# Four query buffers in place of two in a two-branch attention kernel, with a re-dealt instruction plan

## The chip, the cores and the metric

The kernel runs on one core of a Trainium2 chip. The metric is the device time of one execution in microseconds (us). The kernel before took 821.07 us, the median of 7 runs (819.73 to 822.99).

## What is computed

The input x is 2048 tokens by 512 features, bf16. Two attention branches of 32 heads of 16 features each read it; a gate mixes their outputs.

```python
g = sigmoid((x * gate_w).sum(-1))
# A: softmax attention
q, k, v = split(x @ A_wqkv)                       # 32 heads x 16
o = softmax(q k^T * 16**-0.5) v
a = o @ A_wo
# B: linear attention with the softmax feature map phi(u) = [softmax(u w_phi), softmax(-u w_phi)]
q, k, v = split(x @ B_wqkv)
kv, z = phi(k)^T v, sum(phi(k))
b = ((phi(q) kv) / (phi(q) z + 1e-6)) @ B_wo
out = g * a + (1 - g) * b
```

Branch A is nearly all of the work: 32 heads x 2048 x 2048 exponentials.

## The kernel before

**Rounds.** Branch A's work is cut into 32 rounds, numbered n: four chunks of 512 queries by eight groups of four heads. A round has 16 key tiles of 128 keys, and for each key tile four scores (one per head), each a 128 x 512 tile: 64 score tiles in a round.

**Two paths for a score tile.** Of the 16 key tiles of a round, DVE_COUNT[n] (1 to 4) go to VectorE and GpSimd, the others to ScalarE.

- ScalarE's path: two score matmuls (L934, a pair) write two of the four banks of `ps_ring`; one exponential over both (L952) writes two of the NSLOT = 22 slots of the ring ET; four matmuls with the value tile (L991, called PV below) add into `ps_ot`. The score pair k waits for exponential k-2, whose banks it takes. An exponential waits until the PV matmuls that read its slots have run, NSLOT tiles back.
- VectorE's path (`dve_pack`): score matmuls (L1041) into banks of `ps_mp`; VectorE converts them into EW (L1046); the fraction is converted into Ef (L1075, on POOL or VectorE as the plan decides), the exponent into ED (L1079, POOL); VectorE computes a polynomial (L1084, L1086, L1088); a DMA from POOL's queue adds Ef into ED (L1091); four PV matmuls (L1102) read ED.

At the end of a round VectorE transposes `ps_ot` (L1131), divides (L1133, L1134) and, after each second round, transposes into onT_A (L1142).

**Query buffers.** The scores need the queries of a round as four zero-padded planes, one per head, with 16 live rows each. Two rounds share one projection (L775), copied into one of two staging buffers qst (L792); `place_qT` then issues four DMA copies on SP's queue (L810), which put each head's 16 rows into the buffer of that round. There are two such buffers, `qT[:, n % 2]`, cleared once by VectorE at the start (L729). The copies for round n wait for the last score pair of round n-2 (`qk_last`) and for the last VectorE-path score of round n-2 (`qk_dve`), both of which read the same buffer. For the first two rounds VectorE makes the planes itself (L796).

**Branch B and the projections** fill the gaps: features are computed by a projection, two exponentials on ScalarE (phi, L1250), a DMA transpose on SP's queue (phiT, L1285), sums, a reciprocal and products on VectorE. `phi` has six buffers. Outputs of the first three query chunks are projected (L1345), scaled on VectorE into one of three `outt` buffers (L1366) and stored (L1353).

**The order of the work** comes from a planner in the kernel (`Sched`), which runs when the program is built. Each operation has an engine, an assumed duration, a priority and a due time; a greedy loop deals them to the five engines and so fixes each engine's instruction list and every semaphore wait. The tables at the top of the file (LEAD, AFF, PAIR, JOINT, OFF, PRI, SHY, FILL, SLIP, POLY, SHAPE, mostly one value per round) shift priorities, release times and choices in it. Where PE would idle by over 0.26 us in the plan, and fewer than QUOTA = 4700 columns were streamed in the last TICK = 3.413 us of it, the planner puts in spare matmuls (L1010) that multiply a zero tile, so that PE stays busy:

```python
while (self.open and now - t[e] > self.SPARE and
       sum(n for x, n in self.recent if x > now - self.TICK) < self.QUOTA):
    z = self.spare(cfg)
```

Of the kernel before, what the change touches and what calls it, by code (L numbers as in the profile page):

```python
# [11 lines left out]
P = 128  # L12
D = 512
H = 32
DH = 16
S = 2048
NT = S // P
QCH = 512
# [10 lines left out]
NSLOT = 22  # L29

PASSES = 1
LEAD = [30.0, 5.0, 15.587634343078882, 19.4910031759405, 21.09664890476773, 40.82165272376692, 4.700229106743385, 13.0]
PACE = [1.0771457571608845, 0.4579007635970128]
BOUNDS = [3.0710501327799653, 8.000889564597248, 8.026121532808418, 18.02257936663145, 29.86797202712817]
# [4 lines left out]
AFF = [4.39977984498405, 3.9999969024869326, 0.0709056182711651, 2.610626798369437, 0.0, 3.8238247132441265, 0.2373548188763579, 1.6727442850838754, 0.0, 0.6573637706948927, 0.11081142926777193, 1.5407840050620647, 0.0, 3.3884248072966137, 0.44709012098761747, 1.0475205744010385, 0.6221806062526727, 0.0, 0.9703265408840219, 3.181313389852499, 2.9697049628010324, 0.0, 0.4901783546835013, 0.0, 0.0, 2.786126368892715, 1.0743845299433354, 0.7132921107694127, 3.722000841705053, 4.3096284141584125, 0.22230757516151967, 2.6591770654809825, 0.0]  # L39
PAIR = [1, 0, 0, 0, 0, 1, 0, 0, 0, 0, 1, 1, 0, 1, 1, 1, 1, 1, 0, 1, 1, 1, 0, 0, 0, 1, 0, 0, 1, 0, 1, 0, 0]  # L40
JOINT = [0, 0, 1, 0, 0, 0, 0, 1, 1, 1, 0, 0, 0, 0, 0, 0, 1, 1, 1, 1, 1, 1, 1, 1, 0, 0, 0, 0, 1, 1, 1, 1, 0]
SWD = [0.65, 662500, 1.85]
CLEAR = [3.0, 1.2, 0.97, 4.85, 3.2623642462425315, 5.2, 2.6, 0.05]
OFF = [0.0, 0.7641466610336427, 0.5172481291637241, 5.004931148448025, 1.7040388526462977, -7.164186188736442, 0.7559066313969969, 1.9941725662135408, -6.707776703782448, 4.972788778180723, 5.007934767851205, -6.13598057955875, 3.881877451844217, -2.647081027044541, -5.72687170676355, -0.22403507521855937, -4.84468290973168, 4.404669149906992, 7.812513114609348, 3.1840076962397728, -6.5688103099769055, 0.35249872570063623, 3.345678581583612, -4.520043988488846, -1.9086060678527623, 10.430360554436882, 3.604407185155254, -16.81889329298839, 4.746243695454299, -2.846662271061698, 5.685383556076899, 5.689588100027095, 0.0]
PRI = [-2.5977761809841518, 7.675212586195942, 3.895376356683779, 19.79515516194705, -7.3276780691927526, 14.469014115627996, 8.592499852018925, 14.099502747418079, 12.338502872342715, 1.7122892583984095, -8.935875976393678, 0.5395473944292624, 14.23703340786056, 3.2346729790774353, 0.3457488045955195, 0.08236959814205402, -17.48520710204307, -7.161052481135956, -16.754409768115014, -4.23626845606058, 7.608907873204804, -3.2170380366050266, 8.401619955625353, -20.005512559792166, 1.3250396846988832, 4.674069890641421, -7.994912686036253, -4.543452568119845, 2.6005386807691826, -5.230522475232639, -10.205604389261005, 0.3055335737033076, 0.0]
SHY = [0.9001243968886534, 1.8374205889246058, 0.0, 2.3537546061047485, 0.18257087375037662, 1.4295929945532806, 0.0, 0.5036278855954646, 0.6445455027631356, 0.2763577403328745, 1.1375351044326518, 2.139068753246887, 0.8637774561861942, 0.0, 1.3587360146178078, 1.1498488277746914, 4.411308196696776, 1.5770165321690843, 0.0, 1.9277987030895938, 0.9106226852257446, 1.1437315353611544, 0.5739539000045727, 0.1122566866758205, 2.0455679537055595, 0.8660155278776578, 0.6489629968075317, 3.2915775917012993, 0.0, 0.0, 0.1739731045745717, 1.0328008471107046, 0.5]
FILL = [0.008114156552610996, 0.8711172814468358, 0.1337127379043423, 0.6175020065897155, 0.7705201692590595, 0.3506528409175884, 0.2044338913945295, 0.5026251860805567, 0.5, 0.21748892677719284, 0.48467810123534716, 0.3196791772769674, 0.2851905504944167, 0.01919447461597057, 0.15335430645841516, 0.32782401328955907, 0.2084505307424424, -0.011934960453968912, 0.520663695866737, 0.5981936577952663, 0.11372240291845498, 0.6724825225634218, 1.0685006718840102, 0.5449804341491988, -0.3447736801528881, 0.360791111116348, 0.09588691498317847, 0.029755556837955832, 0.29038499291635267, 0.6891067868200518, 0.5206497795807705, 0.1370411081981146, 0.5]
SLIP = [0.020288650601543372, 0.020525550031210083, 0.06075207595460803, 0.0, 0.0, 0.0, 0.13508451326551305, 0.0, 0.024065167618767248, 0.0, 0.015945258750116847, 0.0, 0.002841362237768881, 0.05233800887856601, 0.0, 0.0, 0.0554960908741312, 0.014128492530835347, 0.06406254955060428, 0.01059294453046039, 0.06237810720540699, 0.14637347669762, 0.0, 0.03425975512431642, 0.07117502284429342, 0.0852953029317602, 0.0, 0.016465068465927216, 0.0, 0.11752530161540813, 0.10555114660507484, 0.0, 0.0]
POLY = [2.5698857428809108, 0.8749370011032089, -0.8991089305608342, -3.284378557461031, -2.104961201961929, 2.1622309334875944, -1.9547520224875896, 1.9344506377095603, 0.8679101929667505, 6.980907311200291, 0.597989766211239, 11.29232777066949, 4.7841112088256725, 3.454905016185241, -9.642279457647597, -1.4127995308506685, -1.3053317023544437, -1.7341301539172118, 7.659960632132543, 5.984807460007567, 4.8208000760169565, 0.5343684926269039, 5.3604542710823715, -0.36855426206960495, 0.9175715562645521, 1.9673598560009513, -4.573797529614719, 1.399931277308983, -4.6711373321518534, -0.22371921092667524, 3.420996744961034, 5.649687125694619, 2.3718927004339707]
SHAPE = [0, 1, 2, 0, 3, 2, 1, 0, 0, 4, 0, 0, 3, 0, 0, 3, 0, 0, 1, 1, 0, 0, 1, 1, 3, 0, 1, 2, 0, 0, 1, 4, 1]  # L50
# [11 lines left out]
DVE_COUNT = (1, 3, 4, 3, 3, 3, 2, 2, 1, 3, 3, 4, 2, 4, 3, 3, 3, 3, 4, 3, 4, 3, 2, 4, 3, 3, 3, 3, 3, 3, 3, 4)  # L62
# [61 lines left out]
class Sched:  # L124
# [330 lines left out]
    TICK, QUOTA = 3.413, 4700  # L455
# [56 lines left out]
class _Kernel:  # L512
# [43 lines left out]
    def memory(self):  # L556
# [20 lines left out]
        bf, f32 = dt.bfloat16, dt.float32  # L577
# [22 lines left out]
        at("qT", [P, 2, 4, QCH], bf)  # L600
# [17 lines left out]
        at("outt", [P, 3, D], bf)  # L618
        at("phi", [P, 6, H, 2, DH], bf)
# [9 lines left out]
    def pools(self):  # L629
        self.mp = BufPool(NMP)  # L630
        self.mp.scarce = True
        self.qst_p = BufPool(2)
        self.onTA_p = BufPool(9)
        self.onTB_p = BufPool(9)
        self.EW_p = BufPool(2)
        self.ED_p = BufPool(3)
        self.Ef_p = BufPool(3)
        self.outt_p = BufPool(3)
        self.phi_p = BufPool(6)
        self.VB_p = BufPool(6)  # L640
        self.phiT_p = BufPool(2)
        self.fs_p = BufPool(2)
        self.ob_p = BufPool(2)
# [10 lines left out]
    def bank(self, readers=1):  # L654
        return Buf(self.mp, readers)
# [63 lines left out]
    def consts(self):  # L719
        s = self.s  # L720
# [9 lines left out]
                     for n in range(2)]  # L730
# [8 lines left out]
        for k in range(WARM + 5):  # L739
# [5 lines left out]
            if 0 <= t < 4:  # L745
# [6 lines left out]
                if t % 2:  # L752
# [4 lines left out]
                    else:  # L757
# [7 lines left out]
                             order=[self.o_iden])  # L765
# [38 lines left out]
    def place_qT(self, n):  # L804
        par = n % 2
        st, o_ev = self.st_q[n // 2]

        def put(i):
            r0 = 32 * i + 16 * par
            return lambda e: e.dma_start(self.qT[r0:r0 + 16, par, i, :], self.qst[r0:r0 + 16, st.idx, :])  # L810
        self.o_qT[n] = [self.s.op(
            "sp", 2.45, [put(i) for i in range(4)],
            [o_ev, self.qk_last.get(n - 2), self.qk_dve.get(n - 2), self.o_qz[par]], self.tn(n) - LEAD[4], dma=65536,
            frees=[st])]
        self.o_qT[n][0].lat = 2.3
        self.o_qT[n][0].kind = "qT"
# [63 lines left out]
    def main_chain(self):  # L880
# [28 lines left out]
        for k, (ua, ub) in enumerate(groups):  # L909
# [20 lines left out]
            def qk(x, half):  # L930
                n, kt, i = units[x]
                g = SEQ[n][1]
                r = slice(64 * (i // 2), 64 * (i // 2) + 64) if half else slice(0, P)
                return lambda e: e.matmul(  # L934
                    self.ps_ring[:, x % RING, :], self.kT[r, g // 2, kt * P:(kt + 1) * P],
                    self.qT[r, n % 2, i, :], start=True, stop=True, tile_position=(r.start, 0))
# [82 lines left out]
    def dve_pack(self, n, kt, first_pv):  # L1019
# [19 lines left out]
        def score(i, bank, half):  # L1039
            r = slice(64 * (i // 2), 64 * (i // 2) + 64) if half else slice(0, P)  # L1040
            return lambda e: e.matmul(  # L1041
                bank(), self.kT[r, cp, kt * P:(kt + 1) * P], self.qT[r, n % 2, i, :], start=True, stop=True,
                tile_position=(r.start, 0))
# [392 lines left out]
```

## Time and profile before

The profile is of one execution, whose own time was 823.03 us and whose span (first to last instruction of the core) is 821.2 us.

| what | before |
|---|---|
| median of 7 runs | 821.07 us (819.73 to 822.99) |
| profiled execution, its span | 823.03 us, 821.2 us |
| busy PE / VectorE (DVE) / ScalarE (ACT) / GpSimd (POOL) | 748.8 / 758.5 / 802.4 / 394.9 us |
| exponentials ET (L952), phi (L1250) | 834, 64 |
| spare matmuls (L1010) | 383 |
| start of the first and last ET | 8.8, 812.8 us |

A row of a group reads: line, engine, operation, output<-input by name, partitions x elements and type, count, then busy time in us and the mean ns of one, then the idle time of the engine just before these instructions and what ended it. A row of the timeline has the start and the length of a merged piece in us, and in brackets the idle time ahead of it with its releaser. A row of the chain of waits has start, length and what it was. PE's matmuls overlap, so their durations add to more than the time they hold the engine. DVE is VectorE, ACT ScalarE, POOL GpSimd, SP the queue engine; "SPq" is SP issuing a DMA.

### The profile page before, as it was taken

The page shows a single profiled execution, that of the slowest core. Times are in us where ns is not written, and L with a number is a line of the kernel's source. Part 1 is how long each engine was busy: PE and PEld are TensorE (multiplying, and loading weights), DVE is VectorE, ACT ScalarE, POOL GpSimd, SP SyncE. Part 2 cuts the span into 40 slices and gives each one's busy share as a digit, 9 for nine tenths or more (in the row PEclk, how much of TensorE's full clock was granted, in tenths as well). Part 3 has the DMA queues.
Part 4 walks back from the last instruction along what each step waited for, and adds up shares of the span by engine and source line. Part 5 has one row for each costly group of instructions (what it writes and reads, how often), then busy time and mean ns, then how long its engine had stood idle before and what let it go on. Part 6 is the DMA issues. An engine that isn't in the chain of part 4 may idle for free.

```text
span 821.2 us, 14918 instructions
## 1 busy us (share of the span) xinstructions
PE 748.8 (91%) x5944; PEld 225.4 (27%) x5944; DVE 758.5 (92%) x1124; ACT 802.4 (98%) x906; POOL 394.9 (48%) x435
## 2 busy tenths in 40 slices
PE   8999999999999889898999998888888988888997
PEld 3333232333333223222222222222222222222222
DVE  7999999998699999999999999999799999898893
ACT  6999999999999999999999999999899999999997
POOL 3436434632124546556555455544455555564450
PEclk9999999999999999999999999999799999999999
DMA  5454434353326436246534534445356445444433
GB/s 124 115 103 105 88 74 87 73 111 76 69 54 145 95 78 112 59 100 124 103 81 100 115 82 87 94 93 117 72 104 119 81 88 91 84 77 81 81 71 84
DMA packets 96598, 75.84 MB, mean 92 GB/s; under 512 B 76817, under 2 KB 84369, under 8 KB 96529
## 3 DMA queue, kind: packets, MB, share of 16 engines
q0 software_dynamic: 13680, 49.81, 30.8%
q1 hardware_dynamic: 81360, 24.42, 14.5%
q8 instruction: 47, 0.77, 0.4%
q10 hardware_dynamic: 1488, 0.66, 0.3%
q14 instruction: 23, 0.18, 0.1%
HBM read 3.69 MB, written 2.10 MB: 7 GB/s over the span
## 4 chain that ended last, share of the span: by engine, by line
ACT 81%; DVE 7%; PE 6%; DMA 3%; POOL 1%; issue 1%; SPq 0%; POOLq 0%
ACT ET L952 77%; ACT phi L1250 3%; DVE EW L1046 2%; DMA ED<-Ef 2%; PE ps_ring L934 2%; DMA qT<-qst 1%; PE ps_ot L991 1%; DVE Ef L1088 1%; DVE Em L1084 1%; PE ps_mp L1041 1%; DVE Em L1086 1%; DVE Wp L1182 1%; PE ps_mp L1345 1%; PE ps_mp L775 1%; PE ps_ot L1102 0%
## 5 line engine op out<-in xcount | busy, mean ns | idle before, releaser
L952 ACT ACTIVATE ET<-ps_ring 128x1024 bf16<-128x1024 f32 x834 | 776.4, 1214 | 6.9 <-PE ps_ring L934 4.7
L934 PE MATMUL ps_ring<-qT,kT 64*128 64x512 bf16 x1668 | 328.8, 388 | 55.2 <-ACT ET L952 44.6
L1079 POOL TENSOR_SCALAR ED<-EW 128x512 int16<-128x512 int16 (+2 forms) x240 | 221.6, 951 | 197.3 <-DVE Em L1084 49.9
L1046 DVE TENSOR_SCALAR EW<-ps_mp 128x512 int32<-128x512 f32 (+1 forms) x288 | 237.7, 852 | 24.8 <-PE ps_mp L1041 19.3
L934 PEld LDWEIGHTS ps_ring<-qT,kT 64*128 64x128 bf16 x1668 | 80.5, 93 | 327.6 <-ACT ET L952 311.4
L1091 POOL DMA_DIRECT2D ED<-Ef x95 | 87.5, 924 | 123.3 <-DVE Ef L1088 67.6
L991 PE MATMUL ps_ot<-ET,Vaug 128*17 128x512 bf16 x1668 | 146.7, 385 | 0.0
L1075 POOL TENSOR_SCALAR Ef<-EW 128x1024 f16<-128x1024 uint16 (+1 forms) x93 | 88.4, 951 | 89.9 <-DVE EW L1046 28.2
L1088 DVE TENSOR_TENSOR Ef<-Ef,Em 128x2048 int16<-128x2048 f16 x95 | 120.7, 1271 | 0.6
L1084 DVE TENSOR_TENSOR Em<-Ef 128x2048 f16<-128x2048 f16 x95 | 120.5, 1269 | 0.5
L1041 PE MATMUL ps_mp<-qT,kT 64*128 64x512 bf16 (+1 forms) x380 | 102.3, 385 | 7.9 <-DMA qT<-qst 2.6
L1010 PE MATMUL ps_ot<-zero,iden 64*128 64x512 bf16 (+1 forms) x383 | 88.9, 379 | 0.0
L1075 DVE TENSOR_SCALAR Ef<-EW 128x1024 f16<-128x1024 uint16 (+1 forms) x131 | 79.3, 617 | 0.1
L1086 DVE TENSOR_SCALAR Em<-Em 128x2048 f16<-128x2048 f16 x95 | 68.7, 723 | 0.3
L991 PEld LDWEIGHTS ps_ot<-ET,Vaug 128*17 128x17 bf16 x1668 | 32.0, 87 | 74.3 <-issue 68.1
L775 PE MATMUL ps_mp<-Wp,xT 128*128 128x512 bf16 x128 | 41.6, 385 | 0.0
L1250 ACT ACTIVATE phi<-ps_mp 128x512 bf16<-128x512 f32 x64 | 40.0, 778 | 1.3 <-PE ps_mp L775 1.3
L1102 PE MATMUL ps_ot<-ED,Vaug 128*17 128x512 bf16 x380 | 37.5, 385 | 2.1 <-DMA ED<-Ef 1.9
L775 PE MATMUL ps_mp<-xT,WA 128*128 128x512 bf16 (+1 forms) x128 | 38.5, 378 | 0.6 <-ACT phi L1250 0.3
L1041 PEld LDWEIGHTS ps_mp<-qT,kT 64*128 64x128 bf16 (+1 forms) x380 | 27.1, 94 | 40.8 <-DVE EW L1046 18.7
L1010 PEld LDWEIGHTS ps_ot<-zero,iden 64*128 64x128 bf16 (+1 forms) x383 | 25.9, 94 | 11.3 <-issue 0.3
L1131 DVE STREAM_TRANSPOSE T<-ps_ot 128x512 f32<-128x512 f32 x31 | 21.9, 708 | 2.6 <-PE ps_ot L991 2.5
(93 smaller groups left out, 410.9 us busy)
## 6 DMA issues: line engine op xcount, KB each, us to landing
ED<-Ef POOLq DMA_DIRECT2D x95, 512.0 KB, 4.5
qT<-qst SPq DMA_DIRECT2D x120, 16.0 KB, 1.9
out_dram<-outt SPq DMA_DIRECT2D x12, 128.0 KB, 2.0
WA<-in_A_wqkv_dram SPq DMA_DIRECT2D x3, 384.0 KB, 4.5
phiT<-phi SPq DMA_TRANSPOSE x48, 3.1
WBV<-in_B_wqkv_dram SPq DMA_DIRECT2D x1, 512.0 KB, 4.6
Wp<-in_A_wo_dram SPq DMA_DIRECT2D x1, 512.0 KB, 4.1
WBV<-in_B_wo_dram SPq DMA_DIRECT2D x1, 512.0 KB, 4.9
```

Source lines behind the costliest of these rows:

```text
L775: m = s.op("pe", self.c_mm(n), lambda e, c=c: e.matmul(self.bk(b)[:, 0:n], lhs(c), rhs(c), start=(c == 0), stop=(c == 3)), deps if c == 0 ...
L934: return lambda e: e.matmul(self.ps_ring[:, x % RING, :], self.kT[r, g // 2, kt * P:(kt + 1) * P], self.qT[r, n % 2, i, :], start=True, st ...
L952: self.o_exp.append(s.op("act", w * 0.434 + 0.039, lambda e, b0=b0, s0=s0, w=w: e.activation(self.ET[:, s0:s0 + w, :], self.ps_ring[:, b0: ...
L991: return lambda e: e.matmul(self.ps_ot[32 * i:32 * i + VSL, :], self.Vaug[:, kt, h, :], self.ET[:, (4 * p + k) % NSLOT, :], start=(kt == 0 ...
L1010: return lambda e: e.matmul(self.ps_ot[c:c + nc, :], self.iden[r:r + nr, 0:nc], self.zero[r:r + nr, :], start=False, stop=False, tile_posi ...
L1041: return lambda e: e.matmul(bank(), self.kT[r, cp, kt * P:(kt + 1) * P], self.qT[r, n % 2, i, :], start=True, stop=True, tile_position=(r. ...
L1046: return s.op("dve", dur, lambda e: e.tensor_scalar(self.EW[:, ew.idx, x * QCH:(x + w) * QCH].rearrange("p (b q) -> p b q", b=w) if w > 1 else
L1075: fs = [s.op("pool", U * 8.26e-4 + 0.28, lambda e, c=c: e.tensor_scalar(self.Ef[:, ef.idx, U * c:U * c + U], half(0, dt.uint16, c, U), flo ...
L1079: hs = [s.op("pool", W * 8.26e-4 + 0.165, lambda e, c=c: e.tensor_scalar(self.ED[:, ed.idx, W * c:W * c + W].bitcast(dt.int16), half(1, dt ...
L1084: u = s.op("dve", 1.13, lambda e: e.tensor_tensor(self.Em[:], Ef(), Ef(), ALU.mult), fs + [self.ed_prev], pr, port=True)
L1088: g_ = s.op("dve", 1.13, lambda e: e.tensor_tensor(Ef().bitcast(dt.int16), Ef(), self.Em[:], ALU.mult), [q], pr, port=True)
L1091: v = s.op("pool", SWD[0], lambda e: e.dma_start(out().bitcast(dt.int16), Ef().bitcast(dt.int16), accum_op=ALU.add), [g_] + hs, pr, frees= ...
```

## The change

There are four query buffers in place of two: round n uses `qT[:, n % 4]`, and its copies wait for rounds n-4. The two new buffers are cleared by POOL at the start. To make room, ET has 20 slots in place of 22, `phi` five buffers in place of six, `outt` two in place of three. QUOTA goes from 4700 to 4100. DVE_COUNT moves one key tile from round 3 and one from round 11 to rounds 6 and 30 (95 in all in both). The plan tables get new values in some entries: AFF 9, PAIR 5, JOINT 10, OFF 8, PRI 10, SHY 7, FILL 14, SLIP 12, POLY 9, SHAPE 12 of 33 each, LEAD and BOUNDS one each. The planner's code is the same, so the order of the instructions on every engine is dealt anew. Lines after the clearing of the buffers stand two lower in the changed file (L952 is L954 there).

```diff
-NSLOT = 22
+NSLOT = 20
...
-DVE_COUNT = (1, 3, 4, 3, 3, 3, 2, 2, 1, 3, 3, 4, 2, 4, 3, 3, 3, 3, 4, 3, 4, 3, 2, 4, 3, 3, 3, 3, 3, 3, 3, 4)
+DVE_COUNT = (1, 3, 4, 2, 3, 3, 3, 2, 1, 3, 3, 3, 2, 4, 3, 3, 3, 3, 4, 3, 4, 3, 2, 4, 3, 3, 3, 3, 3, 3, 4, 4)
...
-    TICK, QUOTA = 3.413, 4700
+    TICK, QUOTA = 3.413, 4100
...
-        at("qT", [P, 2, 4, QCH], bf)
+        at("qT", [P, 4, 4, QCH], bf)
...
-        at("outt", [P, 3, D], bf)
-        at("phi", [P, 6, H, 2, DH], bf)
+        at("outt", [P, 2, D], bf)
+        at("phi", [P, 5, H, 2, DH], bf)
...
-        self.outt_p = BufPool(3)
-        self.phi_p = BufPool(6)
+        self.outt_p = BufPool(2)
+        self.phi_p = BufPool(5)
...
         self.o_qz = [s.op("dve", 0.9, lambda e, n=n: e.memset(self.qT[:, n], 0.0), prio=-200 + 101 * n)
-                     for n in range(2)]
+                     for n in range(2)] + [
+            s.op("pool", 2.6, lambda e, n=n: e.memset(self.qT[:, n], 0.0), prio=-97 + n, order=[self.o_iden])
+            for n in (2, 3)]
...
-            return lambda e: e.dma_start(self.qT[r0:r0 + 16, par, i, :], self.qst[r0:r0 + 16, st.idx, :])
+            return lambda e: e.dma_start(self.qT[r0:r0 + 16, n % 4, i, :], self.qst[r0:r0 + 16, st.idx, :])
         self.o_qT[n] = [self.s.op(
             "sp", 2.45, [put(i) for i in range(4)],
-            [o_ev, self.qk_last.get(n - 2), self.qk_dve.get(n - 2), self.o_qz[par]], self.tn(n) - LEAD[4], dma=65536,
+            [o_ev, self.qk_last.get(n - 4), self.qk_dve.get(n - 4), self.o_qz[n % 4]], self.tn(n) - LEAD[4], dma=65536,
             frees=[st])]
```

In the score matmuls (L934, L1041) `self.qT[r, n % 2, i, :]` becomes `self.qT[r, n % 4, i, :]`.

## The prediction

> **What bounds the kernel.** I read the page's busy table first, then the groups, then ScalarE's row of the timeline for its pauses, then the chain of waits through the longest pause, then the table by stretches for the TensorE clock there.
>
> ```profile
> span 821.2 us, 14918 instructions
> ...
> PE 748.8 (91%) x5944; PEld 225.4 (27%) x5944; DVE 758.5 (92%) x1124; ACT 802.4 (98%) x906; POOL 394.9 (48%) x435
> ...
> L952 ACT ACTIVATE ET<-ps_ring 128x1024 bf16<-128x1024 f32 x834 | 776.4, 1214 | 6.9 <-PE ps_ring L934 4.7
> ...
> L1010 PE MATMUL ps_ot<-zero,iden 64*128 64x512 bf16 (+1 forms) x383 | 88.9, 379 | 0.0
> ```
>
> ScalarE is busy 98% of the span with 834 exponentials (ET) and 64 feature exponentials (phi), so only what makes ScalarE pause can be won. The busy share hides some of it: an ET lasts 1214 ns but the next begins sooner. From the trace's start times, the median step from ET to ET is 0.904 us and a phi's 0.478. So 833 x 0.904 + 64 x 0.478 + 0.13 for the two gate exponentials = 783.7 us; from the first ET (8.78) to the last (812.80) are 804.0. ScalarE loses **20.3 us** inside its own stream; 8.8 lie ahead and 8.4 behind. The excess of each step over 0.904 tells where: 4.7 us at 574.6 to 585.7; 0.8 at 626.7; 3.7 in the early part (1.8 at 143.1, 0.7 at 101.3, 0.4 at 159.5, 0.9 in three between 65 and 71); 0.9 at 463; 0.7 at 710; the rest in some hundreds of small ones, of which the largest (0.1 to 0.3 each) stand where one round of queries follows the other.
>
> The longest, first as ScalarE's pauses, then as the chain of waits:
>
> ```profile
> 577.74 1.94 ACT L952 ACTIVATE ET<-ps_ring 128x1024 bf16<-128x1024 f32 x2 [1.88 <-PE ps_mp L1041]
> 580.09 1.02 ACT L952 ACTIVATE ET<-ps_ring 128x1024 bf16<-128x1024 f32 x1 [0.42 <-PE ps_ring L934]
> 581.60 1.02 ACT L952 ACTIVATE ET<-ps_ring 128x1024 bf16<-128x1024 f32 x1 [0.48 <-PE ps_ring L934]
> 582.88 1.02 ACT L952 ACTIVATE ET<-ps_ring 128x1024 bf16<-128x1024 f32 x1 [0.25 <-PE ps_ring L934]
> 584.38 1.02 ACT L952 ACTIVATE ET<-ps_ring 128x1024 bf16<-128x1024 f32 x1 [0.48 <-PE ps_ring L934]
> ```
>
> ```profile
> 569.54 0.34 PE ps_ring L934 x2
> 569.88 0.10 SPq L810
> ...
> 572.50 4.12 DMA qT<-qst
> 576.62 0.05 issue
> 576.66 0.61 PE ps_mp L1041
> ```
>
> A score pair of two rounds earlier ends at 569.88; only then may SP's queue issue the four copies into that round's query buffer; the last lands at 576.62, and PE, idle until then, begins the next round's scores. The 626.7 loss is the same wait (PE idle 0.80 us, released by qT<-qst). Why the ETs stay late until 585.7 is in the table by stretches (columns: PE, weight loads, DVE, ACT and POOL busy, granted clock, DMA share, GB/s):
>
> ```profile
> 572.38:575.80 3.42, 2.32 (x12) 0.50 (x9) 3.42 (x7) 3.42 (x4) 0.52 (x1) 1.00 0.78 155
> 575.80:579.22 3.42, 2.56 (x15) 0.55 (x15) 1.53 (x3) 1.54 (x3) 1.48 (x3) 0.50 0.25 49
> 579.22:582.63 3.41, 3.41 (x17) 0.76 (x13) 2.94 (x6) 2.51 (x3) 1.81 (x3) 0.50 0.59 115
> 582.63:586.05 3.42, 3.42 (x20) 0.89 (x20) 1.56 (x4) 2.44 (x3) 2.36 (x4) 0.50 0.58 115
> 586.05:589.50 3.45, 3.10 (x30) 1.01 (x28) 3.45 (x6) 3.45 (x5) 0.58 (x1) 1.00 0.40 76
> ```
>
> PE's pause halved the granted clock for 10.24 us, and at half clock PE cannot feed ScalarE: of the 4.7 us, 2.3 are the wait and 2.4 its echo.
>
> **The change part by part.**
>
> *Four query buffers.* The copies now wait for the scores of four rounds back, not two. A round is about 26 ETs, 24 us, so what they wait for is long done. In the changed order SP issues nearly all copies two or three rounds at a time, far ahead; the feature transposes behind them in SP's queue find no unfinished wait. Both qT losses go: 4.7 + 0.8. What is late next at 575 is DVE, busy until 576.3 with Ef (L1088); it feeds the other path and holds no ET. I leave the usual loss of a change of round, 0.15 twice: **-5.2 us**. Bounds: 0 (something else is as late) and -5.5.
>
> *Two memsets on POOL at the start, and the start's order.* In the changed order DVE does the kT copy (L840 before) ahead of all four qT products (L796), not between them. Before:
>
> ```profile
> 7.68 0.61 DVE L796 TENSOR_SCALAR qT<-qst,par 128x512 bf16<-128x512 bf16 x2
> 8.21 0.55 DVE L840 CAST kT<-ps_mp 128x384 bf16<-128x384 f32 x1
> 8.78 51.52 ACT L952 ACTIVATE ET<-ps_ring 128x1024 bf16<-128x1024 f32 x56 [1.33 <-PE ps_ring L934]
> ```
>
> The copy needs matmuls that end at about 7.8, so it runs to 8.4, the first two products to 9.0, and the first ET starts 0.7 later, on ScalarE's path. The memsets (128x2048) themselves: POOL's 128x128 memset took 0.20 us and its one-element ones 0.10, so 1.7 us each by the slope and 3.2 by proportion; the strided Vaug memset (2.27 for 512) would make it 9, but these are contiguous. POOL is free from 3.7 to 15.1, so 3.4 to 6.4 us hide there; if they took longer than that, POOL's first Ef conversion would be late, not an ET. If the products on DVE cannot run beside a memset, they begin as late as 10.1 and the cost is 2.4. I take **+1.0**, nearer to 0.7; ends 0.7 and 2.4. The trace before has DVE's own memsets running at 1.30 and 2.37 beside POOL's Vaug memset, 0.91 us each, so it shows no such block, but it has no product beside a POOL memset. [...]
>
> *Plan values and column tiles.* Tiles on the DVE path stay 95 in all: one leaves rounds 3 and 11, one comes to 6 and 30, so ET stays 834. By the changed order DVE does 89 + 26 of the Ef conversions (L1075) in place of 95 + 36: 6 x 0.68 + 10 x 0.41 = 8.2 us go to POOL, which is 48% busy; 12 more single and 6 fewer paired EW conversions cost 12 x 0.60 - 6 x 1.13 = 0.4. DVE gains 7.8 us of air, and 5.6 more in round 3 (about 85 to 110), where the chain of waits runs through DVE from 61 to 94; the later tile falls where DVE sat idle (9.7 us before the last transpose). The early losses come from DVE being behind: bounds 0 and -3.7; I take half, **-1.85**. At the end, the changed PE order uses the last ED just ahead of the last PV group. That group ran at 814.2, the last ED matmuls (L1102) at 810.8, 3.4 earlier; after the last change of round DVE's list is about 1.3 us longer (one more Ef conversion and output scaling), which leaves 2.1: cost 0. Its cover is that 2.1; the other end is a whole landing of ED (4.5 us, the median) later, +2.4.
>
> *Shorter ring (22 to 20).* An ET may start only when the PV matmuls 20 tiles back are done. In the trace before, that would have been violated at 143.1 (by 3.2 us, where ScalarE lost 1.8 anyway) and 147.7 (0.1); everywhere else there is 0.36 or more to spare. So 0 to +1.5; **+0.5**. One phi buffer fewer: 0, as the only phi that paused ScalarE waited for its projection; at most one more such pause, +1.3. One outt buffer fewer: 0, since a store lands in 2.0 us and nothing else waits for it.
>
> *Fewer spare matmuls.* L1010 fills idle PE; by the changed order 235 remain of 383. They lie in PE's idle time: 0 now; their cover is the clock, priced below.
>
> **Sum** against the profiled execution (823.03 us: span 821.2 and 1.8 around it): -5.2 + 1.0 - 1.85 + 0.5 = -5.55, so **817.5 us**. The median of the seven runs, 821.07, is 2.0 lower than the profiled one, about the price of the halved clock (2.4), which may not come in each run; the changed kernel should have neither, so I give 817.5 for its median: 0.44% below.
>
> **Rivals.**
>
> 1. *The gain is taken by a new wait.* One half-clock stretch (2.4), or the upper ends of the start (1.4 more) and the ring (1.0 more), put +2.4 on the forecast: 819.9, within 0.2% of the median (about what a measurement of this kernel can tell from no change: 819.4 to 822.7). For it: all waits are dealt anew. Against: the plan has more air on DVE. Chance 0.20.
>
> 2. *Slower: the clock drops where spares are gone.* The window that lost the clock (572.4 to 575.8) had PE's array streaming columns 31% of it, by the matmuls' starts and sizes; windows cut at the same phase with 40 to 41% (57.0, 374.4, 63.8) kept it. So the point lies between 31 and 40%. Laying the changed order out at 0.904 us a pair gives three places under 36% (near 249, 390 and 537 us); the old order has two (near 253 and 351), which kept the clock, the cut lying otherwise. If all three fall, each with the echo of 2.4 us: 817.5 + 7.2 = 824.7. From the third fall it decides by itself (two give 822.3), or from the second with any other wait of 0.4. Chance 0.15. [...]
>
> 3. *DVE's air clears the early losses wholly*, the small ones at the change of round too (copies ready earlier, DVE's scores earlier): another -1.85 and some 2 of the 8 us of small ones: 813.6. Chance 0.13.
>
> 4. *The copies are early but not the limit*: only the 0.8 and 2.3 us of waiting go and the rest stays: counted in the first.
>
> **Numbers.** Forecast 0.52, between 815 and 819.4. Faster: 0.52 + 0.13 = 0.65; same 0.20; slower 0.15. The range reaches to 813.0 (rival 3 nearly whole, 0.05 beyond) and 823.0 (rival 1 and the start of rival 2; 0.14 beyond).
>
> **What would show it.** Right: no pause of ET released by qT<-qst, and no PE idle on it; the first ET near 9.5 to 9.8; clock 1.00 in all slices; L1010 x235 less what the trace misses; the pause of phi at 143 gone or smaller; DVE near 751. Wrong: clock below 1.00 around 249, 390 or 537; ETs waiting on L991 near the fifth round; a pause before the last transposes of more than 1.7 us after the last ET, with PE waiting on ED<-Ef.

## The result, and the profile after

The changed kernel takes **824.57 us** (median of 12 runs, 822.48 to 826.44), the kernel before 821.08 beside it (31 runs): ratio **1.0042, 95% interval 1.0032 to 1.0053**, so 0.42% slower. Measured again later: 825.27 against 821.41, 1.0049 [1.0030, 1.0067]. The forecast was 817.5, and its range ended at 823.0.

The profiled execution of the changed kernel took 823.75 us, only 0.7 more than the profiled one of before (823.03), which was among that kernel's longest. So these two profiles show where time goes, not the whole 3.5 us between the medians. Its page, the lines that answer to those shown of before, and the first line of the chain that ended last:

```profile
span 821.9 us, 14632 instructions
...
PE 727.0 (88%) x5796; PEld 220.6 (27%) x5796; DVE 762.5 (93%) x1114; ACT 802.5 (98%) x906; POOL 409.7 (50%) x439
...
ACT 74%; DVE 14%; PE 6%; DMA 4%; issue 1%; POOL 1%; SPq 0%; POOLq 0%
...
L954 ACT ACTIVATE ET<-ps_ring 128x1024 bf16<-128x1024 f32 x834 | 777.0, 1198 | 7.4 <-PE ps_ring L936 6.7
...
L1012 PE MATMUL ps_ot<-zero,iden 64*128 64x512 bf16 (+1 forms) x235 | 54.8, 378 | 0.0
```

Spares and ET counts are as forecast. DVE is not: 762.5 us busy where about 751 was forecast, and its share of the chain doubled. Before, that line read:

```profile
ACT 81%; DVE 7%; PE 6%; DMA 3%; POOL 1%; issue 1%; SPq 0%; POOLq 0%
```

The first ET starts at 10.87 (8.78 before), the last at 813.81. So ScalarE's own stream is 802.9 us long, 1.1 less than before's 804.0; the forecast wanted 6.55 less.

**Two VectorE operations are held by GpSimd.** At the start, VectorE's timeline and then GpSimd's:

```profile
4.26 2.91 DVE L735 CAST ind<-m 128x8 bf16<-128x8 f32 x1
4.47 2.70 DVE L757 COPY xT<-ps_mp 128x1024 bf16<-128x1024 bf16 x1
5.32 1.85 DVE L760 COPY xT<-ps_mp 128x512 bf16<-128x512 bf16 x1
```

```profile
3.29 3.85 POOL L731 MEMSET qT<- 128x2048 bf16 x2
```

Before, the cast and the last of these copies read:

```profile
4.26 0.16 DVE L733 CAST ind<-m 128x8 bf16<-128x8 f32 x1
...
5.22 0.42 DVE L758 COPY xT<-ps_mp 128x512 bf16<-128x512 bf16 x1 [0.16 <-PE ps_ring L748]
```

The cast of eight numbers per partition took 0.16 us. Now it stands until 7.17, when the two new memsets (3.29 to 7.14) are over, and the xT copies behind it end at 7.17 too; before, they ended at 5.64. Every projection waits for xT, and PE idles 1.6 us for it before the first. The memsets themselves are quick, 1.95 us each, inside my bounds.

At 66 us the same happens; VectorE's timeline, GpSimd's, ScalarE's:

```profile
65.90 1.86 DVE L1166 TENSOR_SCALAR gden<-gneg 128x16 f32<-128x16 f32 x1
67.79 0.25 DVE L1167 RECIPROCAL gcol<-gden 128x16 f32<-128x16 f32 x1
67.96 1.82 DVE L1048 TENSOR_SCALAR EW<-ps_mp 128x512 int32<-128x512 f32 x3
```

```profile
63.54 4.19 POOL L1081 TENSOR_SCALAR ED<-EW 128x2048 int16<-128x2048 int16 x2 [3.15 <-DVE Ef L1077]
```

```profile
69.40 2.92 ACT L954 ACTIVATE ET<-ps_ring 128x1024 bf16<-128x1024 f32 x3 [1.44 <-PE ps_ring L936]
```

Before:

```profile
67.95 0.52 DVE L1164 TENSOR_SCALAR gden<-gneg 128x16 f32<-128x16 f32 x1
```

Now it ends at 67.76, just behind GpSimd's ED conversion (67.73). The EW conversions wait behind it, they hold ps_mp's banks, PE's score waits 1.57 us for a bank, and the ET behind that starts 1.44 us late (1.73 over its usual step). In the new plan whole-tile ED conversions (128x2048, 2.0 us each on average) are 24, not 18. VectorE was slow beside them elsewhere too: at 732.90 a product T<-T,rinv (L1136), 0.42 us by the median, took 2.11 beside an ED conversion that ran from 732.32 to 734.73. All 33 of these products took 2.6 us more than before, and the 190 operations on Em 3.1 more; the longest of those, 3.00 us at 614.04 (1.22 by the median), had three ED conversions beside it (613.87 to 615.96).

**The queries are still late once.** The chain through 557 us (start, length, what):

```profile
550.35 0.61 DVE qst L794
...
550.98 0.52 SPq L812
...
552.81 4.30 DMA qT<-qst
557.11 0.05 issue
557.16 0.60 PE ps_mp L1043 x2
```

No round is waited for now; the source copy qst is late, since VectorE ran without a break from 538 on. This costs 0.83.

**The clock.** It was at half twice in this execution, for 3.41 us each, at 480.1 and 620.0. Busy time by stretch, columns as in the prediction:

```profile
476.65:480.06 3.41, 2.15 (x24) 0.54 (x20) 3.34 (x5) 3.41 (x5) 0.95 (x2) 1.00 0.77 154
480.06:483.47 3.41, 3.41 (x24) 0.79 (x23) 2.73 (x5) 2.77 (x4) 2.17 (x3) 0.50 0.58 115
```

The first stretch has no PE pause above 0.53 us; PE is only thinly loaded (37% of the array by the starts and sizes of its matmuls, 512 columns at 0.21 us, the step between two spares), and the next stretch runs at half clock.

### The profile page after: what moved, and what is told of

Its sections match the earlier page's. It is cut to its first block, busy times and chain, and to the rows that moved or that the text cites. A ratio compares the mean times of both kernels' runs of the same rounds, so it can differ in the third digit from the quotient of the medians.

```text
span 821.9 us, 14632 instructions
## 1 busy us (share of the span) xinstructions
PE 727.0 (88%) x5796; PEld 220.6 (27%) x5796; DVE 762.5 (93%) x1114; ACT 802.5 (98%) x906; POOL 409.7 (50%) x439
## 4 chain that ended last, share of the span: by engine, by line
ACT 74%; DVE 14%; PE 6%; DMA 4%; issue 1%; POOL 1%; SPq 0%; POOLq 0%
ACT ET L954 71%; DVE EW L1048 5%; DMA ED<-Ef 3%; ACT phi L1252 3%; DVE Em L1086 2%; PE ps_ring L936 2%; DVE Ef L1090 2%; DVE Ef L1077 1%; DVE Em L1088 1%; PE ps_ot L993 1%; PE ps_mp L1043 1%; PE ps_mp L777 1%; DMA qT<-qst 1%; PE ps_ot L1104 0%; DMA phiT<-phi 0%
## 5 line engine op out<-in xcount | busy, mean ns | idle before, releaser
L954 ACT ACTIVATE ET<-ps_ring 128x1024 bf16<-128x1024 f32 x834 | 777.0, 1198 | 7.4 <-PE ps_ring L936 6.7
L1081 POOL TENSOR_SCALAR ED<-EW 128x512 int16<-128x512 int16 (+2 forms) x232 | 224.3, 994 | 190.3 <-DVE Ef L1090 53.6
L1077 POOL TENSOR_SCALAR Ef<-EW 128x1024 f16<-128x1024 uint16 (+1 forms) x103 | 96.1, 933 | 114.1 <-DVE Ef L1090 44.3
L1086 DVE TENSOR_TENSOR Em<-Ef 128x2048 f16<-128x2048 f16 x95 | 122.2, 1286 | 0.4 <-POOL Ef L1077 0.2
L1077 DVE TENSOR_SCALAR Ef<-EW 128x1024 f16<-128x1024 uint16 (+1 forms) x115 | 72.0, 639 | 0.0
L1012 PE MATMUL ps_ot<-zero,iden 64*128 64x512 bf16 (+1 forms) x235 | 54.8, 378 | 0.0
L858 PE MATMUL ps_mp<-WA,xT 128*128 128x128 bf16 x192 | 23.0, 222 | 0.0
```

Of the source, the lines that this page charges most:

```text
L954: self.o_exp.append(s.op("act", w * 0.434 + 0.039, lambda e, b0=b0, s0=s0, w=w: e.activation(self.ET[:, s0:s0 + w, :], self.ps_ring[:, b0: ...
L1077: fs = [s.op("pool", U * 8.26e-4 + 0.28, lambda e, c=c: e.tensor_scalar(self.Ef[:, ef.idx, U * c:U * c + U], half(0, dt.uint16, c, U), flo ...
L1081: hs = [s.op("pool", W * 8.26e-4 + 0.165, lambda e, c=c: e.tensor_scalar(self.ED[:, ed.idx, W * c:W * c + W].bitcast(dt.int16), half(1, dt ...
L1086: u = s.op("dve", 1.13, lambda e: e.tensor_tensor(self.Em[:], Ef(), Ef(), ALU.mult), fs + [self.ed_prev], pr, port=True)
```

## The experiments

Theory at this point: (A) the two held operations are the loss. Rivals: (B) the start is absorbed, because the stream behind waits for VectorE anyway; (C) the missing spares cost clock. Ratios are to the kernel before, timed beside it on the same chip; brackets are 95% intervals.

### The start

e1: the two memsets behind the last query product, as 32-bit words (0.92 us each).

```diff
+        after = self.o_qT[0][3]
+        for o in late:
+            out.remove(o)
+            o.deps.append(after)
```

> The changed kernel with every engine's list as it is, but the two POOL memsets of the new query buffers are issued after the first round's four query products on VectorE, as 32-bit words (half the elements). Theory A (the start): the memsets block VectorE's small copies at 4.3 to 7.1 us; moved, the first ET comes near 9.5 us in place of 10.9 and the median is 1.4 us under the changed kernel: 823.2, ratio to before 1.0026. Theory B (VectorE is behind later on, so a late start is absorbed): the first ET is as early, but the median stays within 0.5 of 824.6, ratio 1.004. Theory C (clock): no change but 0 to -1.4 with the start, clock dips as before.

Measured 823.71, 1.0025 [1.0005, 1.0045]: 0.17% below the changed kernel, with intervals that touch. ind takes 0.16 us again. The first ET is at 10.40 in its profile, not near 9.5; by the clock's records the full clock came at 7.8 us there, at 5.6 in the changed kernel's profile.

e2: besides, the start's order as before (kT copy behind the first two products, third V projection behind the first score pair).

```diff
+        out.remove(self.o_k0)
+        out.insert(out.index(self.o_qT[0][1]) + 1, self.o_k0)
...
+        out[out.index(first) + 1:out.index(first) + 1] = v3
```

> As the run with late memsets, and the first kT copy is put back behind the first two query products, the third value projection behind the first score pair. Theory A: first ET near 8.8 to 9.0, median 2.1 us under the changed kernel: 822.5, ratio 1.0017. Theory B: 824 or more, ratio above 1.0035. What is left above 1.000 is then not the start's.

Measured 823.48, 1.0024 [1.0005, 1.0043]; first ET at 9.06 in its profile. By the ratios the start is worth about 1.5 us of the loss, which speaks against B, though this interval overlaps the changed kernel's; and something else remains.

g3 prices the block alone, in the old order: the kernel before with a third query buffer (g2 below), its new buffer cleared by two 128x2048 memsets where the changed kernel has them.

```diff
-        self.o_qz.append(Op("pool", 0.9, [lambda e: e.memset(self.qT[:, 2].bitcast(dt.uint32), 0)], ...))
+        self.o_qz += [Op("pool", 2.6, [lambda e: e.memset(self.qT[:, 2], 0.0)], ...) for _ in range(2)]
...
-        k = out.index(self.o_qT[0][3]) + 1
+        k = out.index(self.o_vones) + 1
```

> The same kernel as the run before it but for the clearing of the new buffer: two memsets of 128x2048 bf16 on GpSimd at the start, where the changed kernel has them, in place of one after the query products. Nothing else is moved, so it prices the block alone. Theory (GpSimd's memset holds VectorE's small copy ind and the xT copies behind it): ind takes about 2.9 us, the first ET starts 1.4 later (near 10.2), and the time is 1.4 above the run before it, ratio 1.0017 to that. Rival (the start's delay is absorbed, as the stream behind it waits for other things): first ET 1.4 later, the time equal within 0.3.

Measured 820.23, 0.9985 [0.9971, 1.0000]; g2 beside it 819.51, 0.9987. The medians differ by 0.7, the ratios not at all, so no price of the block shows here. The profile says why it may be small: ind took 1.17, not 2.91. It ended at 5.42, between the start of the two memsets and their end (3.28 and 7.26), and the first ET started at 9.06, no later than in the two profiles of g2 (9.52 and 8.89).

```profile
4.25 1.17 DVE L753 CAST ind<-m 128x8 bf16<-128x8 f32 x1
```

In the four profiled executions with these two memsets at the start, ind took 2.91 twice (the changed kernel, two runs) and 1.17 twice (g3, and e3 below). In the changed kernel's first profile the first memset ends at 5.40, so the 1.17 (to 5.42) fits a cast that got in between the two.

### The gate operation

g1: e2, and gden with its reciprocal moved behind three EW conversions.

```diff
+        out.remove(a)
+        out.remove(g)
+        k = next(k for k, o in enumerate(out) if o.eng == "dve" and o.port and o.start > g.start)
+        out[k:k] = [a, g]
```

> The changed kernel with the start in the old order (as in the second run) and, besides, VectorE's two gate operations (gden and its reciprocal, 128x16) moved three EW conversions later, behind GpSimd's long ED conversion. Theory (each small operation held by a GpSimd operation is on the path): gden takes 0.52 us again in place of 1.86, the pause of ET at 66.7 (1.73 us) goes, and the time is 1.7 below that run: about 821.8, ratio to the kernel before 1.0003. Rival (VectorE is late at that point anyway, and the next wait takes its place): the pause moves or shrinks by under 0.5, about 823.3, ratio 1.002.

Measured 822.34, 1.0015 [1.0001, 1.0029], on another chip than e2. In its profile:

```profile
66.37 0.17 DVE L1208 TENSOR_SCALAR gden<-gneg 128x16 f32<-128x16 f32 x1
```

```profile
63.37 9.43 ACT L996 ACTIVATE ET<-ps_ring 128x1024 bf16<-128x1024 f32 x10
```

Ten ETs in a row where the pause was: the 1.73 us are gone from the stream. Against e2 the ratio fell by 0.7 us and the median by 1.1, and the intervals of e2 and g1 overlap, so this step alone is not shown to pay. Both steps together are: g1's interval lies wholly under the changed kernel's [1.0032, 1.0053], by 2.2 us between the ratios. That is most of the loss; what is left of it is 0.15%.

### The buffer by itself

g2: the kernel before, the order of every engine kept, one more query buffer (three); copies wait for round n-3. (The third outt buffer lies over memory that is free by then.)

```diff
-            [o_ev, self.qk_last.get(n - 2), self.qk_dve.get(n - 2), self.o_qz[par]]
+            [o_ev, self.qk_last.get(n - 3), self.qk_dve.get(n - 3), late[-1]]
```

> The kernel before, with the order of every engine's instructions kept as it was, and a third query buffer alone: copies wait for round n-3. Theory of the prediction (the buffer's wait was the limit): the waits of PE on qT<-qst go, the half clock at 575 with them, 2.5 to 5 us less: 816 to 818.5, ratio 0.994 to 0.997. Rival (SP's queue and the source copy were as late: SP was busy with onT_B until 569.4 when the buffer came free at 569.9): at most 0.5 us per wait, 820.3 to 821, ratio 0.999 to 1.0.

> The kernel before with a third query buffer in the old order, once more, beside the changed kernel on the same chip. If the buffer's wait alone is worth about 2 us: ratio 0.997 to 0.999 again, and with the first twelve runs the interval leaves 1.0 out; if that was chance, 1.0.

Measured 819.51, 0.9987 [0.9970, 1.0004], and again 819.45, **0.9972 [0.9954, 0.9989]**: 1 to 2 us faster than before by the ratios, **the fastest version of this study**, ahead of both kernels. It lies between the two theories. The PE wait for copies at 627 is gone in both its profiles; where the rest of the gain comes from is not shown. Why not more is in SP's queue (profile of g3, which has the same third buffer):

```profile
555.78 13.07 SPq L1305 DMA_TRANSPOSE phiT<-phi  x3
568.90 1.27 SPq L1340 DMA_TRANSPOSE onT_B<-ob  x1
570.22 3.65 SPq L830 DMA_DIRECT2D qT<-qst  x4
```

The buffer is free long before, but the copies stand behind two kinds of transposes until 570.2, as in the kernel before (569.4). In that execution the slowest copy lands after 4.0 us, PE waits 1.6 and the clock halves; in the two profiles of g2 the copies land in 3.0 and 2.6 at most, and PE itself does not wait for them (one weight load does, 0.6 us).

g4: g2, and each round's copies moved in SP's queue to just behind what they wait for.

```diff
+            out.remove(o)
+            k = max(out.index(d) for d in o.deps + o.war) + 1
+            out.insert(k, o)
```

> The run with the third buffer and the old order, and besides each round's four query copies moved in SP's queue to just behind the step that they still wait for (the source copy, or round n-3). Theory (queue place and buffer were the limit together): no PE wait on qT<-qst at 575 and 626, 2.5 to 5 us less than before, 816 to 818.5, ratio 0.994 to 0.997. Rival (the source is late, or the transposes that now stand behind the copies come later and cost as much): 820 to 821.5, ratio 0.999 to 1.0005.

Measured **836.55, 1.0184 [1.0163, 1.0205]**: far off both theories. The chain shows part of why:

```profile
560.58 0.69 DVE qst L817
561.29 0.52 SPq L835
...
566.71 0.59 SPq L835
...
567.34 3.24 DMA phiT<-phi
...
570.63 0.38 PE ps_mp L1328 x8
```

Eight copies of some 0.6 us issue ahead of a feature transpose, PE waits 3.2 us for it, 3.1 again from 583.7, and 1.7 for another until 156.9. With the half clock behind them these three make some 10 of the 17 us; the rest is spread over smaller pauses that were not followed. In SP's list these eight issues (561.29 to 567.30) stand ahead of the transpose: here "earlier" for one transfer was "later" for the next.

### The spares

QUOTA alone; the order of all other instructions stays. e3 is the changed kernel, e4 the kernel before, h1 and k4 are g1, h2 is g2.

```diff
-    TICK, QUOTA = 3.413, 4100
+    TICK, QUOTA = 3.413, 4700
```

> The changed kernel with QUOTA 4700: 394 spare matmuls in place of 235, all other instructions in the same order. Theory C (the clock drops where spares are gone cost the time): granted clock 1.00 throughout, median at least 1.5 us under the changed kernel: 823.1 or less, ratio 1.0025 or less. Theory A or B: within 0.5 us of the changed kernel, ratio 1.0036 to 1.0048.

> The kernel before with QUOTA 4100: 253 spare matmuls in place of 383, all other instructions in the same order. Theory C: slower by 1 to 3 us, ratio 1.0012 to 1.0037, with dips of the granted clock in the profile. Theory A or B: ratio 1.000 within 0.0008.

> The run with the start and the gate operations mended (g1: ratio 1.0015 to the kernel before), with QUOTA 4700 again in place of 4100; the order of all but the spare matmuls is the same. Theory (what is left after the two blocked copies is half clock, and the missing spares cause it: mean granted clock 0.994 over g1's runs, 0.998 over those of the kernel before): clock 0.997 or more, 1.5 to 2 us less than g1, 820.3 to 821, ratio 0.999 to 1.0. Rival (the spares are not the cause, as the changed kernel with QUOTA 4700 alone was slower, not faster): no gain in clock, 822.3 or more, ratio 1.0015 or more.

> The kernel before with a third query buffer (g2: ratio 0.9987), with QUOTA 4100. Theory (fewer spares cost clock in the old order too): clock 0.998 down to 0.995, 1.5 to 2 us more, about 821.3, ratio 1.000 to 1.001. Rival (no effect): 819.5, ratio 0.9987.

> The mended changed kernel (g1: ratio 1.0015) with QUOTA 3500, 51 spare matmuls in place of 235; the rest of the order is the same. With QUOTA 4700 it was slower (1.0052) at lower clock. If in this order spares themselves start the stalls that cost the clock: faster again, 1.000 or less. If the clock needs spares and 4100 is near the best: slower, 1.003 or more.

| kernel | QUOTA | ratio | mean clock over its runs |
|---|---|---|---|
| before / e4 | 4700 / 4100 | 1 / 1.0019 [0.9996, 1.0041] | 0.998 / 0.996 |
| g2 / h2 | 4700 / 4100 | 0.9987 / 1.0007 [0.9988, 1.0026] | 0.998 / 0.997 |
| changed / e3 | 4100 / 4700 | 1.0042, 1.0049 / 1.0058 [1.0031, 1.0085] | 0.995 / 0.992 |
| g1 / h1 | 4100 / 4700 | 1.0015 / 1.0052 [1.0031, 1.0073] | 0.994 / 0.992 |
| g1 / k4 | 4100 / 3500 | 1.0015 / **1.0082 [1.0051, 1.0113]** | 0.994 / **0.971** |

Few spares cost clock: with the 46 that k4's trace shows there are some 14 half-clock stretches a run by the mean clock. In the old order 4100 looks 0.2% worse than 4700, with intervals that touch. But in the new order 4700 is worse too, so C as I put it (the lower QUOTA is the loss) falls: there 4100 is the best of three. Why more spares hurt there is not settled: both profiles with 4700 show a PE wait of 1.4 us for phiT near 533 and a half clock behind it, which those with 4100 don't. But each of these two profiles was its kernel's fastest run, and k4's, with 3500, has half clock there too, without that wait. Why the new order loses the clock oftener than the old (0.994 to 0.995 against 0.998) stays open.

### The other parts

h3: e1 with LEAD to SHAPE, DVE_COUNT and QUOTA of the kernel before (the tables, as the diff of the change shows them, are left out here).

```diff
-    TICK, QUOTA = 3.413, 4100
+    TICK, QUOTA = 3.413, 4700
...
-        at("rz", [P, 2, 32], f32)
+        at("rz", [P, 4, 32], f32)
```

> The changed kernel's structure (four query buffers, ring of 20, five phi, two outt; the two new buffers cleared after the query products) with the plan values, the column tiles and the QUOTA of the kernel before, so the order is dealt anew by the old values (and four rows of rz in place of two). Theory (the new plan values bring the thin stretches, not the buffers): like the old order with a third buffer, 819.5 to 821, ratio 0.9985 to 1.0. Rival (any new deal with this structure loses as much): 822.3 or more, ratio 1.0015 or more.

Measured **860.71, 1.0487 [1.0469, 1.0504]** at clock 1.00 in its profile; the first theory misses by 40 us, and the rival's "or more" covers it only by the letter. The stream has new pauses; in the longest, ScalarE waits 10.0 us for a score pair, until 369.8. The deal depends so strongly on these values that a structure can't be judged under values made for another.

h4: g2 with a ring of 20.

```diff
+            if self.ubs[k] >= 20:
+                o.deps.append(self.o_pv[(self.ubs[k] - 20) // 4])
```

> The kernel before with a third query buffer in the old order (g2: ratio 0.9987), and a ring of 20 in place of 22 slots: each exponential also waits for the PV matmuls 20 tiles back; one score pair near 143 us stands behind them. Theory of the prediction: +0.5 us on g2 (0 to 1.5), 820.0, ratio 0.9993. Rival (the ring never binds, as at 143 ScalarE waits for phi's projection anyway): 819.5, ratio 0.9987.

Measured 821.17, 1.0000 [0.9986, 1.0014]. Against g2's 0.9987 and 0.9972 this is 1 to 2.3 us, with intervals that touch. The pause at 143 grew from 1.76 us to 2.81 in its profile, and the ET there now waits for a PV matmul (L1034), so some 1 us is the ring's, in the old order.

k3: g2, and one ET moved ahead of the phi pair that pauses ScalarE at 143.

```diff
+        for o in between:
+            out.remove(o)
+        k = out.index(b) + 1
+        out[k:k] = between
```

> The third buffer in the old order, and on ScalarE one exponential moved ahead of the pair of phi that waits at 143 us for its projection. The pause there was 1.34 us and 0.4 of it should stay: 0.9 us less than the run beside it, 818.6, ratio 0.997. Rival (PE's next score waits for the phi's bank, so the pause only moves): equal to the run beside it.

Measured 822.27, 1.0006 [0.9988, 1.0025]: slower than g2 (its second interval touches this one), and the pause is 2.32 us instead of 1.76. The rival's outcome, no gain, came, but not by its reason. The moved ET itself stood, for PV matmuls that free its ring slots and that come behind the projection in PE's list:

```profile
147.00 1.02 ACT L1001 ACTIVATE ET<-ps_ring 128x1024 bf16<-128x1024 f32 x1 [1.90 <-PE ps_ot L1040]
```

So at this place the ring of 22 binds too.

### The changed kernel, run by run

> The changed kernel itself, for the granted clock of each of its runs. If the rest of the loss, behind the two blocked copies, is half clock, its runs have 2 to 4 stretches of half clock on average (mean clock 0.992 to 0.996), and those with the fewest take about 821.5; if not, mean clock 0.998 like the kernel before, and time near 824.5 all the same.

Measured 825.27 (824.11 to 827.84), mean clock 0.995, 2.4 half-clock stretches a run (a stretch of 3.41 us lowers the mean by 0.0021); the runs of before have 1.0. But the run with the highest clock (0.999) still takes 824.95, so half clock is not the whole loss. A fit of time against clock over 272 runs (a level for each kernel, one slope for all) gives 0.54 us for each 0.001, so about 1.1 us a stretch, and these levels at full clock (standard errors up to 0.4):

| kernel | at full clock, us | mean clock | clock's share, us |
|---|---|---|---|
| before | 820.4 | 0.998 | 1.2 |
| changed (k1) | 822.9 | 0.995 | 2.7 |
| e1, memsets late | 822.1 | 0.996 | 2.0 |
| e2, and old start | 820.4 | 0.994 | 3.5 |
| g1, and gden moved | 819.2 | 0.994 | 3.3 |
| g2, third buffer, old order | 819.1 to 819.5 | 0.999 | 0.7 |

The start and gden are worth 3.7 us at full clock (822.9 - 819.2). Without them the new order is 1.2 ahead of the old at full clock, but g1 loses 2.1 more to half clock. For the changed kernel itself: 3.7 - 1.2 + 1.5 (2.7 - 1.2 of clock) = 4.0; measured were 3.9 between the medians. That these agree proves nothing, since the levels are fitted to the same runs. The fit is a correlation: at 575 before, a PE pause of 1.76 us stood ahead of 10.24 us of half clock, and in these 2.4 us of further ET pauses, so the split between "stall" and "clock" is less sure than the runs without the two held operations, which stand by themselves. In k1's own profile the one half-clock stretch lies at the start, from 8.2 to 11.6, just behind the 1.95 us that PE idled for xT; the first ET was at 11.89.

## Why the prediction was wrong

The forecast lay 3.6 us under the median of before, and the measurement 3.5 over it.

- **Start, +1.0 (0.7 to 2.4): the term that failed in kind.** I asked whether the products on VectorE could run beside a memset, took the old trace's two pairs of memsets as a sign that nothing is held, and stayed near 0.7. What was held is an operation I never looked at, the 0.16 us cast ahead of the xT copies. The first ET came 2.1 later than before in the first profile, 3.1 in the second (with half clock), 0.9 in e3's, where ind took 1.17. That 2.1 lies inside my bounds is luck: my 2.4 was for products that wait for a memset, which no run shows (here they begin at 9.77), not for the cast. ind ended at 7.17, when GpSimd's memsets had ended at 7.14, and with the memsets behind the products (e1) it took 0.16 again. I had asked about one pair of instructions and should have gone through every VectorE instruction behind which something waits.
- **Query copies, -5.2: the step that failed was "what they wait for is long done" and with it "what is late next holds no ET".** g2, with three buffers in the old order, gives -1 to -2. At 575 the copies stood in SP's queue till 569.4 for a transpose, half a microsecond before the buffer came free; the price I took was that of one unlucky landing and its echo in one execution. In the changed order the next thing late is the source copy (557), since VectorE is late.
- **VectorE's air, -1.85: failed.** The Ef work did move to GpSimd (7.3 us less on VectorE), but VectorE's busy time rose by 4.0: operations held at the start (2.75 us on ind alone), at gden (1.3), among the T products (2.6) and on Em (3.1) fill it again. Busy time that includes being held can't be forecast by counting operations. The pause at 143 went; that at 66.7 took its place, 1.73 against 1.76.
- **Ring, +0.5:** about 1 in the old order, inside the bounds. In the changed kernel's profile no ET waits for a PV matmul.
- **phi, outt, tail at 0:** nothing speaks against it: no phi paused ScalarE in the profile after, and from the last ET to the end it took 8.1 us, 8.4 before.
- **Fewer spares, 0 now, clock as a rival:** the rival's kind was right and its places were not. Not 249, 390 and 537, but 480 and 620 in one execution and others in the next: what decides it is not shown. Its 824.7 for the slower side is near the measured time by luck, as it comes of another sum. The forecast itself took the changed kernel to run without half clock; its runs had 2.4 stretches each, before's 1.0, which is 1.5 us by the fit. The bound "between 31 and 40%" is no sharp point: a stretch at about 35% (g1, 59.1) kept the clock, one at 38.3% (g1, 349.2) lost it, and so did, in the changed kernel's profile, the one ahead of 620.0 (from 616.6 on) at about 41%. The clock also fell at 480 without a PE pause above 0.53 us.
- **Signs I named:** an ET pause by qT<-qst is left at 557, the first ET is not at 9.5 to 9.8, the clock is not 1.00. Right: 235 spares, the phi pause at 143 gone.

## What to carry to other kernels

When work is added to GpSimd, go through every VectorE operation that will lie beside it, the tiny ones first, and price what queues behind them: 0.16 us of work held 1.5 us of the start. Price a removed wait by what else holds the same transfer (its queue, its source) and from more than one execution; one profile's longest pause may be its worst luck. And where a planner deals everything anew, try the one edit in the old order first: here that alone was 1 to 2 us faster, and the re-dealt kernel 3.5 slower.

## What the runs showed of the hardware that was not expected

- A VectorE cast of 128x8 and an add of 128x16, both reading fp32 from SBUF, stood until GpSimd's memset or conversion ended (2.91 and 1.86 us for 0.16 and 0.17 to 0.52 of work); between two memsets VectorE got in in two of four profiles (1.17).
- The first ET of the same start lay anywhere from 8.8 (before) to 10.9 (g4, where nothing at the start was changed and the full clock came at 10.0 instead of 5.8). Full clock and first ET in other profiles: 4.5 and 8.84 in g1, 7.2 and 9.52 in g2, 7.9 and 9.89 in k3.
- Half clock came to every version, in stretches of 3.41 us (480 and 620 in the changed kernel) or three times that (575 before); by the mean clock there were 0.5 to 4 a run (6 in g4, 14 in k4), and it goes with much of the spread between runs: before's runs without one took 818.7 to 822.4, all its runs 818.7 to 828.2.
